# Attention, channel mix and gated MLP in one kernel: the output projection by seven block products, with sums on VectorE and GpSimd

## The chip, the cores and the metric

The kernel runs on one core of a Trainium2 chip. The metric is the device time in microseconds (us) of one execution, the median of several. TensorE multiplies, VectorE and ScalarE do the elementwise work and read TensorE's banks (PSUM), GpSimd does some elementwise work out of SBUF, and SyncE (SP) issues the DMAs.

## What is computed

Three layers, one behind the other, for 4 batches of 576 tokens (8 heads of 64, width 512, inner width 1024), all in FP32:

```python
# 1. causal attention with a forget bias
scores = q @ k.T / 8 + min(-(cum[:, None] - cum[None, :]), 0)   # cum: running sum of max(s, 0)
attn = exp(scores - rowmax);  attn /= attn.sum(-1) + 1e-9
x = attn @ v                                    # heads side by side: 4 x 576 x 512
# 2. channel mix (x_prev: the token before)
xk = mu_k * x + (1 - mu_k) * x_prev;  xr = mu_r * x + (1 - mu_r) * x_prev
x = sigmoid(xr @ w_r) * (relu(xk @ w_k) ** 2 @ w_v)
# 3. gated MLP
h = gelu_tanh(x @ w_in);  u, v = split(h)       # 512 and 512
v_n = (v - mean) / sqrt(var + 1e-6) * g_ln
v_s = w_sg @ v_n + b_sg                         # over the 576 tokens
out = x + (u * v_s) @ w_out
```

## The kernel before

**Precision.** A product in FP32 is made of three in a reduced form: each operand is split into a high half (a cast, mostly on ScalarE, `copy` at L71) and a low half (operand less high half, mostly on VectorE, `minus` at L74), and TensorE adds high by high, low by high and high by low in one PSUM bank (`mm3` L687, `mm3_steps` L674). Activations have channels on the 128 partitions and tokens along the row, and a tile of 288 tokens (half a batch, `HD`) is what one matmul streams: 128x128 weights, 288 columns.

**Attention and channel mix** run woven into each other up to about 510 us. `attend()` is a generator over 20 jobs, a job being two heads; `moe1()` is one over eight units of 288 tokens. The main loop takes steps of attention in proportion to the matmuls that `moe1` has given out. Both give their work priorities, and a scheduler that runs ahead of time sets each engine's order by them, so the order on an engine isn't that of the code. In attention, `scores` (products L359, L360) puts out scores that VectorE reduces to a row's extreme (L374) and ScalarE exponentiates (L400); `values` transposes, splits the result (`pth` on ScalarE, L545, `ptl` on VectorE, L546) and multiplies by the values (`av`, L527). For the twelve later jobs the division by the row sums comes last: `reciprocals` (L479) adds 1e-9 on GpSimd, inverts on VectorE and sends the row to DRAM, `spread` (L491) fetches it over 128 partitions by DMA (`rb`), and `scale` (L507) multiplies the job's 128x576 output `xt` by it on VectorE, one operation. `mix` (L599) then reads `xt`, first on ScalarE (L610). In `moe1` a unit makes keys (`wk`), the receptance (`wr`, with a tanh on ScalarE into `rt`, L651), turns it into a sigmoid by 0.5 * rt + 0.5 on VectorE (L657) and multiplies by `wv`'s products (L663). The result goes to DRAM (`x2_d`).

**The last stage** has four batches, in a fixed order by code (L975 to L988): `v_side` (v in token rows, GELU, mean and variance), the projection of the batch before, `u_side` (u in channel rows), `norm`, loading x of the next batch (`x_load`), `gate`. The projection of the last batch stands alone at the end. `gate` multiplies the normalised v by the spatial weights (`wg`, with 14 matmuls of 288 columns for each of eight blocks: 4 channel groups d, 2 token halves), scales and adds a bias on VectorE (L930), multiplies by u (L931) and splits into `gh` and `gl`. `project` (L936) makes eight outputs of 128 channels x 288 tokens; each takes 12 matmuls, 4 channel groups by 3, then a VectorE addition of x (L943) and a store. The weights `w_out` are converted from DRAM words to the two halves (`convert` L105, four pieces, bit operations on VectorE) between the first `norm` and the first `x_load` in the code (L982). PSUM in this stage is six banks, used in turn (`ps_b`, L842).

Of the kernel before, what the change touches and what calls it, by code (L numbers as in the profile page):

```python
# [22 lines left out]
P = 128  # L23
# [22 lines left out]
ENG = {"ia": "P", "mx": "D", "ca": "D", "p0": "P", "cl": "D", "qh": "D", "ql": "D", "kh": "A", "kl": "D", "vh": "A", "vl": "D", "xh": "A", "xl": "D", "fh": "A", "fl": "D", "rs": "D", "bh": "A", "bl": "D", "nh": "D", "nl": "D", "gh": "A", "gl": "D"}  # L46
# [6 lines left out]
def block_kernel(ctx: ExitStack, tc: tile.TileContext, qkv, vb, s, w_r, w_k, w_v, mu, w_in, w_out, w_sgT, g_ln, b_sg, out):  # L53
# [51 lines left out]
    def convert(w, c, n, t):  # L105
# [11 lines left out]
        nc.vector.scalar_tensor_tensor(ti, lw, 29, ti, ALU.logical_shift_right, ALU.bitwise_or)  # L117
        half = pool.tile([P, 2, 512], F32R, tag=name, name=name)
        copy("A" if att is not None else "D", half[:, 0], t)
        minus(ENG["cl"], half[:, 1], t, half[:, 0])  # L120
# [386 lines left out]
    def scale(w):  # L507
        nc.vector.tensor_tensor(w.xt[:, 1:], w.xt[:, 1:], w.rb, ALU.mult)
# [87 lines left out]
    def moe1():  # L596
# [29 lines left out]
        for u in range(2 * B):  # L626
# [30 lines left out]
            (nc.gpsimd if ENG["rs"] == "P" else nc.vector).tensor_scalar(rt, rt, 0.5, 0.5, ALU.mult, ALU.add)  # L657
            tc.cur_priority -= PM
            for m in range(4):
# [3 lines left out]
                nc.vector.tensor_tensor(rt[:, m], pm[:, 0:HD], rt[:, m], ALU.mult)  # L663
# [136 lines left out]
    def x_load(b):  # L800
        pool = pb if b % 2 else w2
        xf = pool.tile([P, 4, S], F32, tag="xf", name="xf")
        for hf in range(2):
            nc.sync.dma_start(xf[:, :, hf * HD : (hf + 1) * HD], x2_d[b][hf])
# [4 lines left out]
        xs[b] = xf, xh, xl, x4  # L809
        yield  # L810
        for c in range(4):
            copy(ENG["bh"], xh[:, c], xf[:, c])
            minus(ENG["bl"], xl[:, c], xf[:, c], xh[:, c])
            yield
        copy("D", x4[:, :, 0:D], xf[:, :, 4 * P :])
        minus("D", x4[:, :, D:], xf[:, :, 4 * P :], x4[:, :, 0:D])
# [3 lines left out]
    for size in moe1():  # L820
# [17 lines left out]
        if att is None and w2 is None:  # L838
# [5 lines left out]
            temps = w2.tile([P, 5, 512], F32, tag="vt", name="cvt")  # L844
            lws = conversions([(wi, c, n) for n in (1, 0) for c in range(4)], lambda i: temps[:, i % 5])
# [104 lines left out]
    for c, tags in enumerate(SLOTS):  # L950
# [11 lines left out]
        for x in range(2):  # L962
            wg[x].append(halves[x])
# [82 lines left out]
```

## Time and profile before

| | us |
|---|---|
| median of 3 runs | 701.81 |
| those runs, lowest and highest | 699.28, 704.09 |
| the profiled execution | 701.87 |
| its span, first to last instruction | 700.0 |
| TensorE busy in the span | 666.8 |
| VectorE busy | 535.2 |
| ScalarE busy | 425.0 |
| GpSimd busy | 33.1 |

The span is what the rows of the trace are counted in; the execution's own time is a little longer. The mean granted clock of TensorE is 0.992 of full speed. PE is TensorE's matmuls, PEld its weight loads (they overlap), DVE is VectorE, ACT ScalarE, POOL GpSimd, SPq the queue of SP. L12 is line 12 of the kernel.

### The profile page before, as it was taken

Reading aid. Unit: us, or ns where it says so; the run is one execution under the profiler, and the core shown is the slowest. Engines: PE = TensorE matmul, PEld = TensorE weight load, DVE = VectorE, ACT = ScalarE, POOL = GpSimd, SP = SyncE. Lnnn points to the kernel's source line nnn. Section 1 sums busy time; section 2 is a strip of 40 time slices with the busy share of each in tenths; the row PEclk is TensorE's granted clock in tenths of the full one; section 3 lists DMA queues with packets and bytes.
Section 4 is the critical chain, followed back from the end, with each engine's and each line's share of the span. In section 5 each row is a group of like instructions: output and inputs, shape, how many; then the busy total and the mean of one; then the engine's idle time right before and its main releaser. Section 6 shows DMA issues by size and latency. Waiting matters only on the chain.

```text
span 700.0 us, 12906 instructions
## 1 busy us (share of the span) xinstructions
PE 666.8 (95%) x4638; PEld 620.8 (89%) x4638; DVE 535.2 (76%) x1341; ACT 425.0 (61%) x1011; POOL 33.1 (5%) x86
## 2 busy tenths in 40 slices
PE   7799888999998999999999999999999999999998
PEld 4578866988888989988999999999998998998997
DVE  8999899898989899899887796743847564564543
ACT  5789797778868986896895745725523233133120
POOL 6122100000000000000000000000000000000000
PEclk9999999999999999999999999999999999999999
DMA  8894442352443333423202700004240300300101
GB/s 267 238 286 152 148 137 63 92 154 80 126 118 101 90 109 93 133 81 108 85 22 79 272 10 35 1 18 163 67 112 18 119 1 15 122 2 9 60 1 68
DMA packets 39831, 67.47 MB, mean 96 GB/s; under 512 B 6908, under 2 KB 23400, under 8 KB 39736
## 3 DMA queue, kind: packets, MB, share of 16 engines
q1 hardware_dynamic: 39768, 66.66, 31.2%
q8 instruction: 36, 0.59, 0.4%
q14 instruction: 27, 0.22, 0.1%
HBM read 51.85 MB, written 10.19 MB: 89 GB/s over the span
## 4 chain that ended last, share of the span: by engine, by line
PE 64%; DVE 19%; ACT 6%; DMA 4%; issue 3%; SPq 2%; DVEq 0%; POOL 0%; ACTq 0%
PE m L677 25%; PE po L690 7%; PE pu L690 7%; DVE pr L374 3%; PE pg L925 2%; PE pg L926 2%; PE pg L924 2%; DMA rb<-rd 2%; DVE qk L74 2%; PE pv L863 2%; PE pv L862 2%; PE pv L861 2%; PE av L527 2%; DVE ptl L546 2%; ACT pr L400 2%
## 5 line engine op out<-in xcount | busy, mean ns | idle before, releaser
L400 ACT ACTIVATE pr<-pr,nm 128x448 f32<-128x448 f32 (+4 forms) x144 | 85.1, 592 | 21.2 <-DVE nm L374 20.6
L677 PE MATMUL m<-xh,wk 128*128 128x288 f32 x512 | 83.2, 301 | 0.0
L677 PE MATMUL m<-kh,wv 128*128 128x288 f32 x512 | 79.1, 297 | 0.0
L677 PEld LDWEIGHTS m<-xh,wk 128*128 128x128 f32 x512 | 73.1, 191 | 1.8 <-ACT xh L71 0.7
L677 PEld LDWEIGHTS m<-kh,wv 128*128 128x128 f32 x512 | 71.5, 188 | 0.4
L374 DVE CUSTOM_DVE_ANT_0 pr<-s,mask 128x448 f32<-128x448 f32 (+4 forms) x144 | 64.9, 453 | 8.3 <-PE s L360 6.5
L359 PE MATMUL s<-qk 128*128 128x288 f32 (+4 forms) x144 | 46.8, 327 | 8.6 <-DVE nh L374 5.9
L71 ACT CAST xh<-xf 128x288 fp32r<-128x288 f32 (+1 forms) x80 | 36.1, 480 | 22.7 <-DVE xf L616 10.7
L677 PE MATMUL m<-xl,wk 128*128 128x288 f32 x256 | 47.4, 301 | 0.0
L545 ACT CAST pth<-t 128x512 fp32r<-128x512 f32 (+1 forms) x72 | 38.2, 532 | 13.4 <-PE t L542 12.3
L360 PE MATMUL s<-qk 128*128 128x288 f32 (+4 forms) x144 | 44.1, 309 | 1.8 <-DVE kl L74 1.8
L546 DVE TENSOR_TENSOR ptl<-t,pth 128x512 fp32r<-128x512 f32 (+1 forms) x72 | 43.9, 614 | 2.2 <-ACT pth L545 1.9
L677 PE MATMUL m<-kl,wv 128*128 128x288 f32 x256 | 44.2, 299 | 0.0
L638 ACT ACTIVATE kf<-m 128x288 f32<-128x288 f32 x64 | 26.2, 411 | 28.7 <-PE m L677 28.2
L74 DVE TENSOR_TENSOR xl<-xf,xh 128x288 fp32r<-128x288 f32 (+1 forms) x80 | 39.0, 508 | 5.7 <-PE m L677 4.2
L71 ACT CAST gh<-gf 128x288 fp32r<-128x288 f32 x32 | 13.9, 433 | 45.8 <-DVE gf L931 45.8
L542 PE MATMUL t<-ident,pr 128*128 128x128 f32 x252 | 40.0, 277 | 1.6 <-DVE ptl L546 1.0
L677 PE MATMUL m<-xh,wr 128*128 128x288 f32 x256 | 40.8, 298 | 0.5 <-ACT kf L638 0.3
L610 ACT ACTIVATE xf<-xt,mu 128x288 f32<-128x288 f32 x64 | 33.4, 535 | 12.2 <-DVE xl L74 8.3
L690 PE MATMUL pu<-xh,wi 128*128 128x288 f32 x256 | 39.9, 295 | 0.0
L690 PE MATMUL po<-gh,wk 128*128 128x288 f32 x256 | 39.3, 296 | 0.0
L359 PEld LDWEIGHTS s<-qk 128*128 128x128 f32 x144 | 27.3, 190 | 12.9 <-DVE nh L374 8.1
(299 smaller groups left out, 1738.9 us busy)
## 6 DMA issues: line engine op xcount, KB each, us to landing
kld<-qkv SPq DMA_DIRECT2D x28, 288.0 KB
qld<-qkv SPq DMA_DIRECT2D x24, 288.0 KB
x_d<-rt SPq DMA_DIRECT2D x8, 576.0 KB
xf<-x_d SPq DMA_DIRECT2D x8, 576.0 KB
outT<-ot SPq DMA_DIRECT2D x32, 144.0 KB
vld<-qkv SPq DMA_DIRECT2D x24, 160.0 KB
qk<-qk SPq DMA_DIRECT2D x24, 144.0 KB
rb<-rd SPq DMA_DIRECT2D x24, 128.0 KB
```

What stands on the lines that cost most here:

```text
L71: nc.scalar.copy(dst, src) if eng == "A" else nc.vector.tensor_copy(dst, src)
L74: (nc.gpsimd if pick(engines) == "P" else nc.vector).tensor_tensor(dst, a, b.bitcast(F32), ALU.subtract)
L359: nc.tensor.matmul(dst, qk[0][:, 0, qs], qk[0][:, 1, ks], start=True, stop=False)
L360: issued[0] = nc.tensor.matmul(dst, qk[1][:, 0, qs], qk[1][:, 1, ks], start=False, stop=True)
L374: nc.vector.tensor_tensor_reduce(out=dst, in0=src, in1=msk, scale=-0.125, scalar=first, op0=ALU.add, op1=ALU.min, accum_out=acc)
L400: i = nc.scalar.activation(dst, dst, AF.Exp, bias=nm[:, col : col + 1], scale=-1.0, accum_out=w.sm[:, col : col + 1])
L542: issued[0] = nc.tensor.transpose(bank[:, o : o + P], x, ident)
L545: nc.scalar.copy(pth[:, cols], bank[:, 0:o])
L546: nc.vector.tensor_tensor(ptl[:, cols], bank[:, 0:o], pth[:, cols].bitcast(F32), ALU.subtract)
L610: nc.scalar.mul(xf, xp, mu1[:, j, c : c + 1])
L677: i = nc.tensor.matmul(dst, w(x, c, m), xx[:, c], start=(n + c == 0), stop=(n == 2 and c == w.nk - 1))
L690: nc.tensor.matmul(dst, w(x, c, m), xx[:, c], start=(n + c == 0), stop=(n == 2 and c == w.nk - 1))
```

## The change

- **Projection.** The 512 channels of the gated tile are taken as two halves, its 576 tokens as two halves, and the 512 outputs as two halves: a 2x2 by 2x2 block product. It is made with seven block products instead of eight (Winograd's form): `p11`, `p12`, `p22` and four with sums of weights (`s1` to `s4`). A block product has 256 channels, 256 outputs and 288 tokens, 2 row blocks x 6 matmuls. `quarters` assembles `w_out`, folds the sums of weights once and splits them; it stands behind the first `gate` in the code. `gate` makes the differences of gated blocks (`less`) and splits them too (`halves`, into `tp`). The sums of products are additions on VectorE (`add`) out of PSUM. x is fetched once more for each output, by DMA, into five rotating `ot` tiles; the first addition to it is on GpSimd, and in the last batch's second row block on VectorE. In the last batch x is fetched whole into `xr`. The projection of batch 0 moves behind `u_side`, `norm` and `x_load` of batch 1; those of batches 1 and 2 stay where they were.
- **Norm.** The square root's activation and its table loads go. A bit trick and three Newton steps on VectorE take their place. The casts of the normalised v (`nh`) move from VectorE to ScalarE, as does the cast for `x4`.
- **Receptance.** `wv` is split at half its value, the operation at L657 goes, and the product becomes (rt + 1) * pm, one operation with three operands on VectorE. The GELU table is asked for ahead of time, once.
- **Softmax scaling.** `scale` runs on GpSimd.
- **Loading x.** `x_load` fetches half a batch at a time into one buffer, and converts two channel groups at once; the spatial weights of the last two token groups are loaded behind the first `u_side` instead of ahead of the stage.

```diff
 def convert(w, c, n, t):            # its first part is now assemble(w, c, n, t)
-        copy("A" if att is not None else "D", half[:, 0], t)
-        minus(ENG["cl"], half[:, 1], t, half[:, 0])
+        if w is wv:
+            nc.scalar.mul(half[:, 0], t, 0.5)
+            nc.vector.scalar_tensor_tensor(half[:, 1], t, 0.5, half[:, 0].bitcast(F32), ALU.mult, ALU.subtract)
...
     def scale(w):
-        nc.vector.tensor_tensor(w.xt[:, 1:], w.xt[:, 1:], w.rb, ALU.mult)
+        nc.gpsimd.tensor_tensor(w.xt[:, 1:], w.xt[:, 1:], w.rb, ALU.mult)
...
-            (nc.gpsimd if ENG["rs"] == "P" else nc.vector).tensor_scalar(rt, rt, 0.5, 0.5, ALU.mult, ALU.add)
...
-                nc.vector.tensor_tensor(rt[:, m], pm[:, 0:HD], rt[:, m], ALU.mult)
+                nc.vector.scalar_tensor_tensor(rt[:, m], rt[:, m], 1.0, pm[:, 0:HD], ALU.add, ALU.mult)
...
     def x_load(b):
+        for hf in range(2):
+            hs = slice(hf * HD, (hf + 1) * HD)
+            xf = w2.tile([P, 4, HD], F32, tag="xf", name="xf")
+            nc.sync.dma_start(xf, x2_d[b][hf])
             yield
+            for c in (slice(0, 2), slice(2, 4)):
+                copy(ENG["bh"], xh[:, c, hs], xf[:, c])
+                minus(ENG["bl"], xl[:, c, hs], xf[:, c], xh[:, c, hs])
+                yield
...
     def norm(b, vt, mv):
-        nc.scalar.activation(rs, var, AF.Sqrt)
-        nc.vector.reciprocal(rs, rs)
+        nc.vector.tensor_scalar(rs.bitcast(I32), var.bitcast(I32), 1, 0x7FFFFFFF, ALU.logical_shift_right, ALU.bitwise_xor)
+        nc.vector.tensor_scalar(rs, rs, 0.33885 * 2.0**-64, None, ALU.mult)
+        for _ in range(3):
+            nc.vector.tensor_tensor(t1, rs, rs, ALU.mult)
+            nc.vector.scalar_tensor_tensor(t1, t1, -0.5, var, ALU.mult, ALU.mult)
+            nc.vector.scalar_tensor_tensor(rs, t1, 1.5, rs, ALU.add, ALU.mult)
...
     def gate(b, ut, vh, vl, v4):    # behind the scale and bias of each block (d, hf)
+                if d < 2 and hf:
+                    nc.vector.tensor_tensor(tf[:, 0, c], gf, ut[d // 2][:, d % 2, hs], ALU.mult)
+                    less(tf[:, 1, c], tf[:, 0, c], last)
+                    halves(1, c, tf[:, 1, c])
+                    continue
+                nc.vector.tensor_tensor(gf, gf, ut[d // 2][:, d % 2, hs], ALU.mult)
+                if d >= 2:
+                    if hf:
+                        less(tf[:, 1, c], gf, tf[:, 1, c])
+                        less(tf[:, 0, c], gf, tf[:, 0, c])
+                    else:
+                        less(tf[:, 1, c], gf, tf[:, 1, c])
                 copy(ENG["gh"], gh[:, d, hs], gf)
                 minus(ENG["gl"], gl[:, d, hs], gf, gh[:, d, hs])
+                if d >= 2:
+                    for k, x in ((2, 1), (3, 0)) if hf else ((4, 1),):
+                        halves(k, c, tf[:, x, c])
+                last = gf
...
-    def project(b, xf, gh, gl):     # the eight outputs, 12 matmuls each
+    def project(b, gh, gl):
+        def part(a, x):
+            dst = ps_b.tile([P, 512], F32, tag="b", name="p" + a)[:, 0:HD]
+            for y, z in ((0, 0), (1, 0), (0, 1)):
+                for c in range(2):
+                    nc.tensor.matmul(dst, wq[a][:, y, c, ms], x[z][c], start=(n == 0), stop=(n == 5))
...
+        def emit(i, hf, u, bank):
+            if last:
+                ot = xr[:, i, hs]
+            else:
+                ot = pool.tile([P, HD], F32, tag="ot", name="ot", bufs=n)
+                nc.sync.dma_start(ot, x2_d[b][hf][:, i])
+            (nc.vector if last and m else nc.gpsimd).tensor_tensor(ot, ot, u, ALU.add)
+            add(ot, ot, bank)
+            nc.sync.dma_start(out[b, i * P : (i + 1) * P, hs], ot)
+
+        for m in range(2):
+            ms = slice(m * P, (m + 1) * P)
+            u1, u2 = place(0), place(1)
+            nc.scalar.copy(u1, part("11", block(0, 0)))
+            add(u2, u1, part("s2", tp[2]))
+            emit(m, 0, u1, part("12", block(1, 0)))
+            u3 = place(2)
+            add(u3, u2, part("s3", tp[3]))
+            p5 = part("s1", tp[1])
+            emit(2 + m, 1, u3, p5)
+            add(u2, u2, p5)
+            emit(m, 1, u2, part("s4", block(1, 1)))
+            emit(2 + m, 0, u3, part("22", tp[4]))
...
     for b in range(B):
         vt, mv = v_side(b, xh, xl, x4)
-        if b:
+        if b > 1:
             project(*tail)
...
+        if b == 1:
+            project(*tail)
         gh, gl = gate(b, ut, vh, vl, v4)
+        if b == 0:
+            quarters(last)
```

The order of instructions shows it at three places. The first is VectorE in attention, around a scaling of one of the last full jobs, before (`xt` is the job's output, `rcp` the reciprocals of the next):

```order
L74 TENSOR_TENSOR xl<-xf,xh 128x288
L374 ISA pr_91,nh<-s,mask 128x288
L374 ISA nh 128x1
L508 TENSOR_TENSOR xt_3630<-xt_3630,rb 128x576
L483 RECIPROCAL rcp<-sm 128x9
L74 TENSOR_TENSOR xl<-xf,xh 128x288
```

The same stretch of VectorE in the changed kernel, where L492 is the reciprocal, L383 the reduction and L555 the low half of the transposed scores:

```order
L492 RECIPROCAL rcp<-sm 128x9
L74 TENSOR_TENSOR xl<-xf,xh 128x288 x2
L74 TENSOR_TENSOR kl<-kf,kh 128x576
L555 TENSOR_TENSOR ptl<-t,pth 128x384
L383 ISA pr_91,nh<-s,mask 128x288
L383 ISA nh 128x1
```

The scaling is gone from VectorE; on GpSimd it alternates with the additions of 1e-9 to the row sums, and nothing else stands there in this stretch.

The second place is TensorE at the start of the last batch's projection, before, with the last matmul of the gate ahead:

```order
L928 MATMUL pg<-wg_6338,v_8223 128x288
L690 MATMUL po<-gh,wk_6601 128x288
L690 MATMUL po<-gh,wk_6609 128x288
L690 MATMUL po<-gh,wk_6617 128x288
```

These go on to 96. In the changed kernel `p_` is a product with a plain quarter of the weights, `ps_` one with a sum, and `tp` and the `wg` operands hold the split differences:

```order
L955 MATMUL pg<-wg_6551,v_8408 128x288
L988 MATMUL p_8611<-gh,w_6829 128x288 x4
L988 MATMUL p_8611<-gl,w_6829 128x288 x2
L988 MATMUL ps_8619<-tp,ws_6851 128x288
L988 MATMUL p_8627<-gh,w_6832 128x288
L988 MATMUL ps_8637<-wg_6305,ws_6844 128x288
L988 MATMUL ps_8645<-gh,ws_6839 128x288 x4
L988 MATMUL ps_8645<-gl,ws_6839 128x288 x2
L988 MATMUL ps_8656<-gh,ws_6848 128x288 x4
L988 MATMUL ps_8656<-gl,ws_6848 128x288
L988 MATMUL ps_8619<-tp,ws_6851 128x288 x3
```

There are 84 of them, and products whose operands are ready early are taken ahead of those on the last differences.

The third place is VectorE's end, before:

```order
L931 TENSOR_TENSOR gf<-gf,ut 128x288
L74 TENSOR_TENSOR gl<-gf,gh 128x288
L943 TENSOR_TENSOR ot<-po,xf 128x288 x8
```

and in the changed kernel, where L993 is an addition out of PSUM and L1014 one in SBUF:

```order
L1014 TENSOR_TENSOR xr<-xr,us 128x288 x2
L993 TENSOR_TENSOR xr<-ps_8710,xr 128x288
L993 TENSOR_TENSOR us<-ps_8710,us 128x288
L993 TENSOR_TENSOR xr<-p_8731,xr 128x288
L1014 TENSOR_TENSOR xr<-xr,us 128x288
L993 TENSOR_TENSOR xr<-ps_8721,xr 128x288
```

Eight additions became chains of additions, the last of which need the sum made just ahead of them.

## Rows read from the trace of the kernel before

**Rows 1.** The page: busy us (share) and instructions; the chain by engine.

```profile
PE 666.8 (95%) x4638; PEld 620.8 (89%) x4638; DVE 535.2 (76%) x1341; ACT 425.0 (61%) x1011; POOL 33.1 (5%) x86
...
PE 64%; DVE 19%; ACT 6%; DMA 4%; issue 3%; SPq 2%; DVEq 0%; POOL 0%; ACTq 0%
```

**Rows 2.** Busy time by stretch: length; PE, PEld, DVE, ACT, POOL; clock; DMA; GB/s.

```profile
120.00:385.00 265.00, 253.97 (x1835) 239.62 (x1836) 234.03 (x602) 212.20 (x537) 7.32 (x20) 1.00 0.33 98
583.00:636.00 53.00, 53.00 (x361) 50.46 (x360) 30.02 (x70) 14.99 (x29) 0.00 (x0) 1.00 0.14 46
```

**Rows 3.** The chain of waits in order of time, at its end: start, us, what.

```profile
683.89 12.81 PE po L690 x96
696.73 0.46 DVE ot L943
```

**Rows 4.** Waits of PE, 120 to 385 us: idle us, how often, the longest.

```profile
PE s L359 <- DVE nh L374: 5.9, 8, 1.7
...
PE av L527 <- DVE ptl L546: 2.7, 4, 1.6
```

**Rows 5.** Line L508: shortest/mean/longest ns, first and last; waits before; who waits.

```profile
L508 DVE TENSOR_TENSOR xt<-xt,rb x12: 751/760/764, 144.6 to 386.2; 128x576 f32<-128x576 f32 x12
...
  DMA rb<-rd: 4.3, 7
...
  ACT xf L610: 3.7, 3
```

**Rows 6.** Timeline of VectorE and TensorE around two scalings: start, us, what, [idle before].

```profile
166.24 0.76 DVE L508 TENSOR_TENSOR xt<-xt,rb 128x576 f32<-128x576 f32 x1 [0.68 <-DMA rb<-rd]
...
167.53 0.44 PE L527 MATMUL av<-ptl,vv 128*128 128x384 f32 x1 [0.53 <-DVE ptl L546]
...
302.22 0.76 DVE L508 TENSOR_TENSOR xt<-xt,rb 128x576 f32<-128x576 f32 x1 [0.82 <-DMA rb<-rd]
...
303.93 0.39 PE L527 MATMUL av<-ptl,vv 128*128 128x256 f32 x1 [1.55 <-DVE ptl L546]
```

**Rows 7.** Lines L657 and L663, as rows 5.

```profile
L657 DVE TENSOR_SCALAR rt<-rt x8: 702/751/762, 127.5 to 493.9; 128x1152 f32<-128x1152 f32 x8
...
L663 DVE TENSOR_TENSOR rt<-m,rt x32: 396/456/459, 131.8 to 505.9; 128x288 f32<-128x288 f32 x32
```

**Rows 8.** Lines by form on GpSimd: busy us, mean ns | idle before, by whom.

```profile
L482 POOL TENSOR_SCALAR sm<-sm 128x9 f32<-128x9 f32 x12 | 5.9, 492 | 206.3 <-ACT pr L400 206.3
...
L454 POOL TENSOR_SCALAR pr<-pr,rc 128x128 f32<-128x128 f32 x4 | 4.1, 1014 | 5.0 <-DVE rc L412 3.1 <-PE t L472 1.3 <-PE t L438 0.6
...
L74 POOL TENSOR_TENSOR qk<-qld,qk 64x256 fp32r<-64x256 f32 x4 | 3.5, 890 | 20.1 <-DMA vb<-vb 8.0 <-issue 6.1 <-ACT qk L71 6.0
```

**Rows 9.** Timeline of GpSimd and VectorE, 54 to 61 us.

```profile
54.97 1.88 POOL L74 TENSOR_TENSOR qk<-qld,qk 64x256 fp32r<-64x256 f32 x2 [7.98 <-DMA vb<-vb]
...
56.18 1.21 DVE L117 SCALAR_TENSOR_TENSOR cvt<-wr20w,cvt 128x512 int32<-128x512 int32 x1
...
59.90 0.68 DVE L117 SCALAR_TENSOR_TENSOR cvt<-wr30w,cvt 128x512 int32<-128x512 int32 x1
```

**Rows 10.** Timeline of VectorE in a gate of the last stage.

```profile
525.70 0.45 DVE L931 TENSOR_TENSOR gf<-gf,ut 128x288 f32<-128x288 f32 x1
526.07 0.51 DVE L930 SCALAR_TENSOR_TENSOR gf<-pg,g_sb,b_sb 128x288 f32<-128x288 f32 x1
526.65 0.46 DVE L74 TENSOR_TENSOR gl<-gf,gh 128x288 fp32r<-128x288 f32 x1
```

**Rows 11.** Lines of ScalarE, 385 to 700 us, as rows 8.

```profile
L894 ACT ACT_TABLE_LOAD x4 | 5.1, 1283 | 0.1
```

**Rows 12.** Timeline of VectorE, SP's queue and ScalarE at loads of x.

```profile
516.60 0.29 DVE L71 CAST x<-xf 128x256 fp32r<-128x256 f32 x1 [10.22 <-DMA xf<-x_d]
...
606.88 1.20 SPq L804 DMA_DIRECT2D xf<-x_d  x2
...
613.18 2.40 ACT L71 CAST xh<-xf 128x576 fp32r<-128x576 f32 x4 [1.85 <-DMA xf<-x_d]
```

More of the change, by code (lines that the diff above doesn't have):

```diff
@@ L656, in moe1 @@
             tc.cur_priority += PM
-            (nc.gpsimd if ENG["rs"] == "P" else nc.vector).tensor_scalar(rt, rt, 0.5, 0.5, ALU.mult, ALU.add)
+            if not more:
+                nc.scalar.activation(first, rt[:, 3, 0:1], AF.Gelu_apprx_tanh)
             tc.cur_priority -= PM
@@ L852, in v_side @@
     def v_side(b, xh, xl, x4):
-        vt = w2.tile([P, 5, DM], F32, tag="vt", name="vt")
+        vt = value_rows("vt")
         mv = mvs[b % 2]
@@ L880, in u_side @@
     def u_side(b, xh, xl):
-        ut = pb.tile([P, 4, S], F32, tag="ut", name="ut")
+        ut = [pb.tile([P, 2, S], F32, tag=f"ut{k}", name=f"ut{k}") for k in range(2)]
+        last = []
         for m in range(4):
@@ L913, in norm, with halves, less @@
         return vh, vl, v4
+    def halves(k, c, x):
+        copy("A", tp[k][0][c], x)
+        minus("D", tp[k][1][c], x, tp[k][0][c])
+    def less(dst, a, b):
+        nc.vector.tensor_tensor(dst, a, b, ALU.subtract)
     def gate(b, ut, vh, vl, v4):
@@ L948, in block_kernel, with spatial @@
         nc.gpsimd.memset(mv[:, 4], 1.0)
-    wg = [[], []]
-    for c, tags in enumerate(SLOTS):
+    wg, pieces = [[], []], []
+    def spatial(c, pool, tag, last=None):
+        tags = SLOTS[c]
         if len(tags) == 2:
-            halves = [w1p.tile([P, S], F32R, tag=t, name=f"wg{c}") for t in tags]
+            place = [w1p.tile([P, 1024], F32R, tag=t, name=f"wg{c}") for t in tags]
+            pieces.extend(x[:, S : S + HD] for x in place)
+            place = [x[:, 0:S] for x in place]
@@ L961, in block_kernel @@
-            minus("D", halves[1][:, hs], raw, halves[0][:, hs])
+            i = nc.scalar.copy(place[0][:, hs], raw)
+            if last is not None:
+                behind(i, last[7])
+            minus("D", place[1][:, hs], raw, place[0][:, hs])
         for x in range(2):
-            wg[x].append(halves[x])
+            wg[x].append(place[x])
+    for c in range(3):
+        spatial(c, mw, "xf")
     wo = Weight(w1p, "wk", w_out)
-    temps = w1p.tile([P, 2, 512], F32, tag="wk01", name="cvt")
@@ L966, in block_kernel, with quarters, split, fold @@
-    cos = conversions([(wo, i, 0) for i in range(4)], lambda i: temps[:, i % 2])
+    wq = {}
+    def quarters(last):
+        ta = w1p.tile([P, 2, 512], F32, tag="wk01", name="cvt")
+        tb = w1p.tile([P, 2, 512], F32, tag="wr30", name="cvt")
+        for c in range(4):
+            load_words(wo, c, 0)
+        for c in range(4):
+            assemble(wo, c, 0, (ta, tb)[c // 2][:, c % 2])
+        a11, a21, a12, a22 = (t[:, :, i * 256 : (i + 1) * 256] for t in (ta, tb) for i in range(2))
+        def split(name, pool, tag, x):
+            w = wq[name] = pool.tile([P, 2, 2, 256], F32R, tag=tag, name="w" + name)
+            behind(nc.scalar.copy(w[:, 0], x), last[5 if name[0] == "s" else 3])
+            minus("D", w[:, 1], x, w[:, 0])
+        def fold(dst, x, y, op):
+            nc.vector.tensor_tensor(dst, x, y, op)
+        split("11", w1p, "wk00", a11)
+        split("12", w1p, "wk10", a12)
+        split("22", w1p, "wk20", a22)
+        fold(a22, a21, a22, ALU.add)
+        split("s1", w1p, "wk30", a22)
+        fold(a21, a11, a21, ALU.subtract)
+        fold(a11, a22, a11, ALU.subtract)
+        split("s3", xtp, "xh", a21)
+        fold(a12, a12, a11, ALU.subtract)
+        split("s4", xtp, "xl", a12)
+        split("s2", w1p, "wr30", a11)
```

109 lines of the change are left out of this document (64 added, 45 removed).

## The prediction

> **What bounds the kernel now.** I read the page's busy shares and chain first, then busy times by stretch, then the waits of the stretch in which TensorE is not full. TensorE is busy 666.8 of 700.0 us and is 64% of the chain of waits, VectorE 19% [rows 1]. By stretch [rows 2] there are two kernels in one. In attention (120 to 385 us) TensorE is busy 254.0 of 265 us and VectorE 234.0: both are nearly full, and TensorE's 11 idle us there stand mostly behind VectorE (5.9 us before the scores, waiting for the reduction of the scores before them, 2.7 us before `av`) [rows 4]. From 385 us on TensorE is full and everything else is slack: in one batch of the last stage, 583 to 636 us, it is busy 53.00 of 53 us, VectorE 30.0, ScalarE 15.0, GpSimd 0. The projection there is one piece of the chain, 96 matmuls in 12.81 us, 0.1334 us each, and after the last of them stand only one VectorE addition of 0.46 us and its store [rows 3]. So in the last stage a matmul less is 0.133 us less, as long as nothing else becomes late; in attention what counts is VectorE's time.
>
> **The change part by part.** The sum is made against the profiled execution: span 700.0 us, 701.87 us as a whole, so 1.87 us lie around it; the median of the runs is 701.81 us, the same within 0.1 us.
>
> *Seven products for eight.* Before, one batch is 4 x 2 outputs of 12 matmuls, 96. After, it is 7 products x 2 row blocks x 6 matmuls, 84, of the same 128x128x288 form. 12 x 0.1334 = 1.60 us a batch, four batches: **-6.4 us**, if TensorE stays full.
>
> *What pays for it on VectorE, in the batches that are not the last.* The gate gets 14 more VectorE operations a batch (8 differences, 6 low halves), the projection 6 more (14 additions for 8). One 288-column operation follows another after 0.37 us (525.70 to 526.07), a scale-and-add after 0.58 us [rows 10]: 20 x 0.37 = 7.4 us. Newton's five more operations of 5 columns and the four casts that go to ScalarE about cancel. VectorE goes from 30.0 to some 38 us, TensorE from 53.0 to 51.4. That is still covered, with 13 us of slack. GpSimd gets 8 additions of 288 columns. Their price is not in the trace; nearest are 9 columns in 0.49 us on average and 64x256 in 0.89 us, both two plain forms [rows 8]; from these 288 columns take about 0.94 us (0.89 + 32 x 0.40/247), 7.5 us a batch. Even if VectorE stood still for all of it, it would have 45.5 us of 51.4. The cover is gone only beyond 5.9 us more. But a bank of PSUM is held until a GpSimd sum is there, and in these stretches single waits may come out: I take **+0.5 us** for three batches, 0 to 5 as bounds (0: all under the six banks; 5: each batch gives back its 1.6 us).
>
> *Batch 0.* The w_out conversion moves behind the gate in the code, and its four foldings and three more low halves come to VectorE; the order puts most of it still ahead of the gate's first result. Before, VectorE idles 10.22 us there, waiting for x. x now comes in two halves through one buffer, the second load only after the first is converted: before, in a later batch, both halves were issued by 608.1 us and converted from 613.18 us on [rows 12], so a load takes about 5 us and two in a row 10. The project of batch 0 is moved behind the second u-side, which leaves VectorE 12.8 us more. I cost it at nothing; the work that hides it is the gate's and v-side's 27 us of TensorE; without that cover it is up to 5 us, one load.
>
> *The square root.* Two table loads a batch of 1.283 us go [rows 11]; ScalarE is idle 38 of 53 us, so they are worth 0.
>
> *The last batch.* Here the cover ends. In the order rows TensorE issues 32 matmuls, 4.27 us, behind the gate before it needs the cast of the last gate block, and 53 matmuls, 7.1 us, before it needs the very last operand (`tp`, low). VectorE has 24 operations for the gate's second half, 20 x 0.37 + 4 x 0.58 = 9.7 us, and TensorE takes 56 x 0.133 = 7.5 us for it; VectorE can only start on each block when it is there, so it ends some 2.2 us late, plus two sums of `us` and the last block's own chain, about 5 us behind the gate's end for the last operand, 4.1 us for the cast. 4.1 against 4.27 us: just covered, and one GpSimd addition in between (0.94 us) uncovers it. Behind the last matmul there are now three VectorE additions instead of one: 2 x 0.4 = 0.8 us more. I take 0.8 + 0.5 = **+1.3 us**, bounds +0.5 and +4.
>
> *Scaling and receptance in attention.* VectorE loses 12 scalings of 0.760 us (9.1 us) and 4.3 us of standing before them for the row sums' DMA [rows 5], and eight `rt` operations of 0.751 us, six of them before 385 us (4.5 us); 24 of the 32 products with `rt` become the three-operand form, by the rows 0.52 for 0.456 us, +1.5 us [rows 7, 10]. That is 16.4 us of VectorE's 234, if GpSimd took nothing from it. It does take something: during the second of two GpSimd subtractions, 1.88 us together, a VectorE operation that otherwise takes 0.68 us took 1.21 us [rows 9], 0.53 us more for 0.94 us of GpSimd, about half. A 576-column scaling on GpSimd costs, from 0.89 us at 256 and 0.49 at 9 columns, 1.41 us; the lower bound is 0.89 us, the upper one, by the 128-column operation with a row's scalar (1.014 us), 4.6 us. I take 1.5, since it is the same plain form as the 0.89 us row. If VectorE stands half of it again, 12 x 0.75 = 9 us come back, and 7.4 us are left. What of it reaches TensorE is read from single places: after the scaling at 302.22 us (0.82 us wait) TensorE idles 1.55 us before `av`, after that at 166.24 us 0.53 us [rows 6]. These 2.1 us go, and of the other 9 us idle behind VectorE I take a tenth: **-3 us**. Bounds: -8 (nearly all of that idle time goes) and +7 (below).
>
> The Trainium skill says of this, in "SBUF — State Buffer" (SBUF: two separate sides), that GpSimd and VectorE share a pair of SBUF ports, and that whichever starts first holds it for its whole instruction against a VectorE operation with two SBUF inputs or in a two-port mode. The stretched row agrees. By that rule a scaling can hold VectorE for all of its 1.5 us and not for half, and the sum in attention would be 1.6 us of VectorE's time lost where I have 7.4 us won, or about 0 us in place of -3.
>
> *Sum.* 700.0 - 6.4 + 0.5 + 1.3 - 3.0 = 692.4 us span, + 1.87 = **694.3 us**, 1.1% under the median.
>
> **The rivals.**
> (A) As summed, 694.3 us, own range 691 to 698. For it: TensorE's full stretches and the counted matmuls.
> (B) VectorE is the real bound of attention, and all the relief reaches TensorE: -8 instead of -3, 689.3 us. For it: nearly all of TensorE's idle time there is behind VectorE. Against: after a removed wait the next engine (ScalarE, 212 of 265 us busy) is close.
> (C) The hold eats the relief in attention: 0 instead of -3, 697.3 us.
> (D) The last stage gives the projection's gain back, PSUM banks waiting for GpSimd's sums behind VectorE's norm: +5 instead of +0.5, 698.8 us. Against: 13 us of VectorE slack a batch.
> (E) Slower: the scaled tile comes late. GpSimd scales at twice or more my price, held up by VectorE as VectorE is by it. The mixing on ScalarE waited 3.7 us for three of the twelve scalings already [rows 5]. At 3 us a scaling these waits grow by 2.2 us each, 6.7 us over three, and VectorE loses 12 x 3.0 against 13.4 us won, 22 us, of which a third on the path is 7.5 us: -6.4 + 1.8 + 6.7 + 7.5 = +9.6, 711.5 us. It decides from about 2 us a scaling on; at 1.5 us it does not exist. Against: the 0.89 us row.
>
> **How the numbers follow.** About 1% (7 us) is what a measurement of this kernel can tell from no change. Chances: A 0.38, B 0.24, C 0.18, D 0.11, E 0.09. Faster by over 1% is under 694.8 us: B, and a little over half of A (0.22): 0.46. Slower is most of E: 0.07. The rest, 0.47, is the same. The predicted time is A's. The range reaches from B's, 1.3 us lower for the unknown in its size, to D's with 4 us for C and D together: 688 to 703; outside are E and the far end of B.
>
> **What would show it.** Of the changed kernel: TensorE at 84 matmuls a projection, 11.2 us, and no idle time in the last three batches but under 0.5 us each (D wrong). In the last batch under 1 us idle between the gate and the end, and three VectorE additions behind the last matmul. VectorE near 38 us in a batch. The GpSimd scalings at 1.3 to 1.7 us, and no VectorE wait for the row sums' DMA. TensorE's idle time from 120 us to the end of attention down from 11 to about 8 us, and attention over some 3 us earlier. I am wrong if the scalings take over 2 us, if the gaps in the last stage add up to more than 3 us, or if attention ends later than before.

## The result

| kernel | us, median (lowest to highest) | runs | against before, 95% interval |
|---|---|---|---|
| before, beside it | 700.96 (699.28 to 704.09) | 4 | |
| changed | 690.12 (689.22 to 694.87) | 4 | 0.9863 (0.9826 to 0.9899) |
| changed, again, beside experiments | 693.11 (690.91 to 695.70) | 4 | 0.9881 (0.9847 to 0.9915) |

The change takes 1.2 to 1.4% off, 9.5 us over the eight runs (median 692.0, against 701.5 over 43 further runs of before); 7.5 had been forecast. For the second four a median of 690 to 692 had been expected. The profiled execution of the changed kernel took 689.22 us, span 687.4 us.

One thing has to be known to read the numbers. One program's executions differ by up to 6 us, and most of it goes with TensorE's mean granted clock. In this profile it is 0.997, in that of before 0.992; before shows 0.94 in three of the first four stretches of 30 us, the changed kernel in one of them, and in the rest of both nearly all is at 1.00, the upper of its two levels (2.4 GHz). Over all runs of all kernels below, a line gives 3.5 us for 0.01 of mean clock. So below each kernel has, beside its median, its time on that line at a clock of 0.990. By that, before is 701.9 us (+-0.2) and the changed kernel 692.0 (+-0.4): 9.9 us. A +- is one standard error here and below. It leaves out that executions taken at different times differ by more than that: the two groups of four of the changed kernel lie 2.0 us apart on the line, and before, measured beside the last four kernels of the table below, 1.0 us under before beside the others. Differences of 1 to 2 us by the line alone are therefore weak; the times of whole stretches of the trace, below, are stronger.

The changed page, busy time and chain (as [rows 1]):

```profile
PE 654.9 (95%) x4590; PEld 612.5 (89%) x4590; DVE 563.2 (82%) x1412; ACT 436.3 (63%) x1058; POOL 80.9 (12%) x126
...
PE 69%; DVE 13%; issue 5%; ACT 5%; DMA 5%; POOL 1%; SPq 1%; DVEq 0%; ACTq 0%; POOLq 0%
```

48 matmuls less, VectorE 28 us more, GpSimd 48 us more, and VectorE's share of the chain down from 19 to 13%. The two stretches of [rows 2] in the changed kernel:

```profile
120.00:385.00 265.00, 258.67 (x1892) 247.45 (x1891) 229.75 (x589) 212.83 (x540) 23.54 (x31) 1.00 0.34 99
583.00:636.00 53.00, 53.00 (x360) 50.27 (x359) 36.95 (x89) 16.25 (x35) 9.76 (x9) 1.00 0.22 68
```

In attention TensorE gets 1892 matmuls done where it had 1835, and idles 6.3 us where it had 11.0. In the last stage it is as full as before, with VectorE at 37 us of 53. What TensorE waits for in attention (120 to 385 us, as [rows 4]):

```profile
PE av L536 <- DVE ptl L555: 4.0, 8, 0.7
PE s L368 <- DVE nh L383: 0.8, 1, 0.8
PE av L536 <- ACT pth L554: 0.7, 2, 0.5
```

The wait ahead of the scores fell from 5.9 to 0.8 us, that ahead of `av` grew from 2.7 to 4.0. The scaling, on GpSimd (as [rows 5]):

```profile
L517 POOL TENSOR_TENSOR xt<-xt,rb x12: 1417/1430/2003, 142.8 to 378.0; 128x576 f32<-128x576 f32 x12
...
  DMA rb<-rd: 11.2, 7
...
  ACT xf L619: 2.2, 4
```

It takes 1.43 us, GpSimd and not VectorE stands before the row sums' DMA, and the mixing waits no more than before (2.2 us for 3.7). The product with three operands, (rt + 1) * pm, takes as long as the one with two did (0.45 us both). The end of the chain (as [rows 3]):

```profile
682.99 0.41 PE p L988 x3
683.41 0.02 issue
683.43 0.46 DVE xr L993
683.89 0.38 DVE xr L1014
684.27 0.02 issue
684.29 0.46 DVE xr L993
```

Three additions stand behind the last product, 1.32 us to the end of the last, against one of 0.46.

The projection can be read without the clock, since the stages from the first gate on run at 1.00 but for the last few microseconds. The line of the gate's high products gives the first and the last start, in the kernel before, the changed kernel and the one with eight products (below):

```profile
L924 PE MATMUL pg<-wg,vh x128: 288/295/300, 509.0 to 683.1; 128*128 128x288 f32 x128
```

```profile
L951 PE MATMUL pg<-wg,vh x128: 288/295/300, 501.1 to 671.3; 128*128 128x288 f32 x128
```

```profile
L949 PE MATMUL pg<-wg,vh x128: 288/295/300, 501.0 to 675.0; 128*128 128x288 f32 x128
```

From the first start to the end of the span (700.0, 687.4 and 691.7 us) that is 191.0, 186.3 and 190.7 us. Over all profiled kernels it is 190.7 to 192.2 us with eight products (five) and 185.3 to 186.8, mean 185.9, with seven (nine). The kernel with eight products has the other edits of the last stage, and they give next to nothing (190.7 for 191.0).

Attention and the rest of the channel mix can be read in the same way, since every kernel here has 3350 matmuls ahead of the first gate. The last 2500 of them, before and changed (from 151.2 and 149.1 us to the first gate; a matmul or two more overlap the edge of the window):

```profile
151.25:509.00 357.75, 346.96 (x2501) 331.03 (x2500) 290.34 (x710) 255.65 (x614) 5.45 (x16) 1.00 0.30 91
```

```profile
149.05:501.05 352.00, 344.84 (x2502) 331.55 (x2501) 282.56 (x690) 255.19 (x621) 21.09 (x27) 1.00 0.31 96
```

The same work takes 5.8 us less. So of the 12.6 us between the two spans, 5.8 lie in this stretch, 4.7 behind it and 2.1 ahead of it, where the granted clock differs.

### The profile page after: what moved, and what is told of

It reads as the page before. It is cut to its first block, busy times and chain, and to the rows that moved or that the text cites. A ratio compares the mean times of both kernels' runs of the same rounds, so it can differ in the third digit from the quotient of the medians.

```text
span 687.4 us, 13039 instructions
## 1 busy us (share of the span) xinstructions
PE 654.9 (95%) x4590; PEld 612.5 (89%) x4590; DVE 563.2 (82%) x1412; ACT 436.3 (63%) x1058; POOL 80.9 (12%) x126
## 4 chain that ended last, share of the span: by engine, by line
PE 69%; DVE 13%; issue 5%; ACT 5%; DMA 5%; POOL 1%; SPq 1%; DVEq 0%; ACTq 0%; POOLq 0%
PE m L687 28%; PE pu L700 7%; PE ps L988 3%; PE av L536 3%; PE t L551 2%; PE pg L952 2%; PE pg L953 2%; PE pg L951 2%; PE p L988 2%; PE pv L876 2%; PE pv L877 2%; PE pv L875 2%; DVE pr L383 2%; PE s L368 2%; PE s L369 2%
## 5 line engine op out<-in xcount | busy, mean ns | idle before, releaser
L383 DVE CUSTOM_DVE_ANT_0 pr<-s,mask 128x448 f32<-128x448 f32 (+4 forms) x144 | 64.7, 453 | 7.9 <-PE s L369 6.8
L1014 POOL TENSOR_TENSOR ot<-ot,u 128x288 f32<-128x288 f32 x24 | 24.8, 1043 | 246.7 <-ACT u L1021 225.9
L74 DVE TENSOR_TENSOR xl<-xf,xh 128x288 fp32r<-128x288 f32 (+1 forms) x80 | 41.8, 540 | 11.2 <-ACT xh L71 6.1
L555 DVE TENSOR_TENSOR ptl<-t,pth 128x512 fp32r<-128x512 f32 (+1 forms) x72 | 44.2, 616 | 2.2 <-ACT pth L554 1.6
L687 PEld LDWEIGHTS m<-xl,wk 128*128 128x128 f32 x256 | 38.1, 189 | 0.3
L687 PEld LDWEIGHTS m<-xh,wr 128*128 128x128 f32 x256 | 36.2, 188 | 2.0 <-ACT kf L647 1.3
```

The source lines that it names most:

```text
L74: (nc.gpsimd if pick(engines) == "P" else nc.vector).tensor_tensor(dst, a, b.bitcast(F32), ALU.subtract)
L383: nc.vector.tensor_tensor_reduce(out=dst, in0=src, in1=msk, scale=-0.125, scalar=first, op0=ALU.add, op1=ALU.min, accum_out=acc)
L555: nc.vector.tensor_tensor(ptl[:, cols], bank[:, 0:o], pth[:, cols].bitcast(F32), ALU.subtract)
L687: i = nc.tensor.matmul(dst, w(x, c, m), xx[:, c], start=(n + c == 0), stop=(n == 2 and c == w.nk - 1))
```

## The experiments

All runs in one table; "idle" is TensorE's idle time from 120 to 390 us in the profile, which holds all of attention in its later part. In half of the profiles the granted clock is 1.00 in all of that stretch; in the other half it is 0.83 to 0.97 in one to four stretches of 10 us. "2500 matmuls" is the time of the last 2500 matmuls ahead of the first gate, less what such stretches cost (1 less the granted clock, times 10 us: 3.4 us in "before + both", the second changed one and "four pieces", 1.7 in "scaling back", "first additions" and "behind each scaling", 0 in the others). It is one execution each; the two of the changed kernel agree within 0.2 us, but where two kernels have one order of instructions in attention (below) they differ by up to 1.3.

| kernel | median us (runs) | at clock 0.990 | idle us | 2500 matmuls us |
|---|---|---|---|---|
| before | 701.5 (43) | 701.9 | 11.0 | 357.8 |
| before + scaling on GpSimd | 699.85 (10) | 700.7 | 10.0 | 356.2 |
| before + half folded into wv | 700.92 (10) | 701.4 | 9.9 | 357.5 |
| before + both | 698.83 (10) | 698.2 | 6.8 | 352.4 |
| changed | 692.0 (8) | 692.0 | 6.3, 6.5 | 352.0, 351.8 |
| changed, scaling back on VectorE | 694.48 (4) | 693.9 | 9.0 | 356.2 |
| changed, receptance as before | 696.32 (5) | 695.4 | 9.2 | 356.3 |
| changed, eight products | 697.41 (7) | 695.5 | 6.8 | 352.6 |
| changed, first additions on VectorE | 692.07 (4) | 692.4 | 6.5 | 352.0 |
| changed, GpSimd operation behind each scaling | 693.91 (4) | 693.9 | 8.2 | 355.3 |
| changed, GpSimd operation ahead of each scaling | 695.02 (4) | 693.5 | 9.1 | 355.4 |
| changed, scaling in four pieces | 695.23 (4) | 693.7 | 7.2 | 353.5 |
| changed, q's low halves on GpSimd too | 690.87 (4) | 689.0 | 6.0 | 350.7 |

The standard error of a value at 0.990 is 0.4 us for ten runs and 0.6 for four.

**The parts of attention, one by one.** The scaling alone, in the kernel before:

```diff
-        nc.vector.tensor_tensor(w.xt[:, 1:], w.xt[:, 1:], w.rb, ALU.mult)
+        nc.gpsimd.tensor_tensor(w.xt[:, 1:], w.xt[:, 1:], w.rb, ALU.mult)
```

> The kernel before, with the softmax scaling alone moved to GpSimd. In the changed kernel the last stage begins 8.1 us earlier than before (first v_side product at 396.5 for 404.6 us). Theory 1, VectorE's time is the bound of attention: the scaling takes 9.1 us of work and 4.3 us of waits off VectorE and gives 4.4 us back where GpSimd's scaling holds it, 9.0 us net of the 12.0 us that the whole change takes off it there, so three quarters of the 8.1 us: the last stage begins 6 us earlier, total about 695. Theory 2, only the waits for the row sums' DMA count: 4.3 us earlier at most, total about 697. Theory 3, the gain is that of a new order that the scheduler happened on, and not of the scaling: no fixed sign, within 2 us of 701.

Measured: 0.9989 of before (0.9968 to 1.0009), 1.2 us at the same clock. Not the 6 us of theory 1. The waits of TensorE, 120 to 390 us, tell where they went:

```profile
PE av L527 <- DVE ptl L546: 5.3, 11, 1.2
PE s L359 <- DVE nh L374: 1.6, 2, 0.8
PE av L527 <- ACT pth L545: 1.4, 4, 0.7
```

The wait ahead of the scores is gone (1.6 for 5.9 us), and the one ahead of `av` has grown by most of that (5.3 for 2.7, and ScalarE's part 1.4 for 0.3). It moved. The longest of these waits, 1.20 us, with VectorE's queue ahead of it:

```profile
311.70 0.81 DVE L74 TENSOR_TENSOR xl<-xf,xh 128x288 fp32r<-128x288 f32 x2
312.44 0.74 DVE L657 TENSOR_SCALAR rt<-rt 128x1152 f32<-128x1152 f32 x1
313.10 0.74 DVE L74 TENSOR_TENSOR qk<-kld,qk 64x576 fp32r<-64x576 f32 x1
313.77 0.68 DVE L546 TENSOR_TENSOR ptl<-t,pth 128x512 fp32r<-128x512 f32 x1
...
314.50 0.39 PE L527 MATMUL av<-ptl,vv 128*128 128x256 f32 x1 [1.20 <-DVE ptl L546]
```

VectorE comes to `ptl` without a gap, and one of the operations ahead of it is the receptance's `rt`. The fold that removes that one, alone (with `wv` split at half its value in `convert`, as in the change):

```diff
-            (nc.gpsimd if ENG["rs"] == "P" else nc.vector).tensor_scalar(rt, rt, 0.5, 0.5, ALU.mult, ALU.add)
...
-                nc.vector.tensor_tensor(rt[:, m], pm[:, 0:HD], rt[:, m], ALU.mult)
+                nc.vector.scalar_tensor_tensor(rt[:, m], rt[:, m], 1.0, pm[:, 0:HD], ALU.add, ALU.mult)
```

> The kernel before, with the receptance's half folded into wv alone (no operation of 0.751 us a unit, three operands in the product). Theory 1, VectorE's time is the bound: it takes 3.0 us net off VectorE in attention, a quarter of the whole, so the last stage begins 2 us earlier, total about 699. Theory 2, only waits count: no wait is removed, 0 us, total 701. Theory 3, a new order: any sign, as large as for the scaling.

Measured: 0.9992 (0.9969 to 1.0016), 0.5 us at the same clock. The scores' wait is as it was (5.2 us). Both together in the kernel before:

> The kernel before with both edits of attention, the scaling on GpSimd and the receptance's half folded into wv; last stage as before. Alone they gave 1 us (699.85 for 701.7) and nothing that can be told (700.9), where 6 and 2 had been expected, and yet TensorE's idle time from 120 to 400 us is 11.0 us before, 6.3 in the changed kernel and 6.8 in the one with eight products. Theory 1, VectorE's time counts, but the two edits only tell together: 5 to 6 us faster than before, about 696, idle 120 to 400 us near 6.5 us. Theory 2, the gain ahead of 400 us belongs to the rest of the change (conversions and loads taken out of the way): about 700, idle near 10 us. Theory 3, to the order that the scheduler found: any of the two, but then the two kernels of the same call that undo one edit each lose as much for reasons of order.

Measured: 0.9961 (0.9937 to 0.9986), 3.7 us at the same clock, idle 6.8 us. Its waits:

```profile
PE av L531 <- DVE ptl L550: 3.5, 7, 0.8
PE av L531 <- ACT pth L549: 1.0, 2, 0.9
PE s L363 <- DVE nh L378: 0.8, 1, 0.8
```

Each alone gives about 1 us of idle time, both 4.2; of the 2500 matmuls' time 1.6 and 0.3 us, both 5.4. Now the same from the other end, the changed kernel with one of them undone (the diffs above, backwards).

> The changed kernel with the softmax scaling back on VectorE. Theory 1 (VectorE's time, both edits needed): most of the gain in attention goes, 4 to 5 us slower than the changed kernel, about 695. Theory 2 (the rest of the change): within 1.5 us of the changed kernel, about 691. Theory 3 (order): between the two, with the loss at single waits of TensorE that do not stand behind the scalings.

Measured: 694.48 us, 1.9 us (+-0.7) slower than the changed kernel at the same clock, idle 9.0 us, the 2500 matmuls 4.2 us longer.

> The changed kernel with the receptance as before: wv split at its whole value, 0.5 * rt + 0.5 as an operation of its own on VectorE, two operands in the product. Theory 1: up to 5 us slower than the changed kernel, about 695 (both edits needed) or 2 us (VectorE's time by its share). Theory 2 (the rest of the change): within 1.5 us, about 691. Theory 3 (order): any value up to 5 us slower.

Measured: 696.32 us, 3.4 us (+-0.7) slower, idle 9.2 us, the 2500 matmuls 4.3 us longer. The waits of these two, in that order:

```profile
PE s L368 <- DVE nh L383: 5.1, 6, 1.7
PE av L536 <- DVE ptl L555: 2.1, 3, 1.1
```

```profile
PE av L532 <- DVE ptl L551: 5.1, 11, 1.2
PE av L532 <- ACT pth L550: 1.6, 3, 1.1
PE s L364 <- DVE nh L379: 1.6, 2, 0.8
```

They are the waits of the two single edits again: with the scaling on VectorE TensorE waits at the scores, with `rt` there and the scaling gone it waits at `av`. That both edits are needed is shown, and theory 2 (the rest of the change) falls: with both in the kernel before, the 2500 matmuls take 352.4 us, as in the changed kernel. Theory 3 (order) is not ruled out by this. The order of instructions on TensorE, VectorE, ScalarE and GpSimd is the same, record for record, up to some 400 us in "before + scaling" and "receptance as before", in "before + fold" and "scaling back", and in "before + both" and "eight products", so that the same waits in both families are no second piece of evidence. The fold alone hardly changes the order before (of 1099 VectorE operations ahead of the first gate 1059 stand in the same sequence), the scaling changes it much (797). How much of the gain is VectorE's time and how much the order that goes with it, these runs don't separate; the kernel with a GpSimd operation behind each scaling (below) has the changed kernel's order on TensorE and VectorE through attention, and there time lost on VectorE is seen to reach TensorE.

**The projection.** Eight products in blocks of 12 matmuls, one addition on VectorE each, nothing else changed:

> The changed kernel with eight block products of 12 matmuls an output and one addition on VectorE for each (no differences in the gate, no sums of weights, no addition on GpSimd); everything else as changed. By the two traces the seven products give 3.7 us over the first three batches and 0.8 us at the end, 4.5 us. If the projection is what does that, this kernel is 4.5 us slower than the changed one, about 694.6 us, with the loss only behind the first v_side, and its attention ends within 1 us of the changed kernel's. Rival: the projection gives next to nothing and the last stage owes its time to the other edits there (norm, loading of x): under 1.5 us slower, about 691.

Measured: 697.41 us, 3.5 us (+-0.6) slower than the changed kernel at the same clock, and 4.4 us by the stages of the two profiles (190.7 for 186.3 us), none of it ahead of the first gate (501.0 and 501.1 us). The 4.5 us hold; against the mean of the nine profiles with seven products (185.9 us) it is 4.8 us. Then where the first addition to x runs:

```diff
-            (nc.vector if last and m else nc.gpsimd).tensor_tensor(ot, ot, u, ALU.add)
+            nc.vector.tensor_tensor(ot, ot, u, ALU.add)
```

> The changed kernel with the first addition to x of each output on VectorE in place of GpSimd, in all batches. Theory, GpSimd's additions cost nothing and save nothing because VectorE has slack in the first three batches: within 1 us of the changed kernel, about 690. Rival, GpSimd's additions (1.04 us each, 24 of them) hold VectorE and PSUM banks: 1 to 2 us faster. Second rival, VectorE becomes late without GpSimd's help: the three projections lose up to 1.6 us each, 2 to 5 us slower.

Measured: 692.07 us, 0.4 us slower at the same clock, less than can be told. From 583 to 636 us TensorE is full either way, VectorE at 37.3 us instead of 37.0. GpSimd's additions neither cost nor save.

**What GpSimd does to VectorE.** In the changed kernel, one scaling beside reductions and low halves that read PSUM, and one beside a low half whose two operands are both in SBUF:

```profile
142.80 1.43 POOL L517 TENSOR_TENSOR xt<-xt,rb 128x576 f32<-128x576 f32 x1 [1.12 <-DMA rb<-rd]
...
142.98 0.51 DVE L383 CUSTOM_DVE_ANT_0 pr<-s,mask,nh 128x288 f32<-128x288 f32 x1
...
143.88 0.68 DVE L595 TENSOR_TENSOR p<-t,p 64x512 fp32r<-64x512 f32 x1 [0.38 <-ACT p L594]
```

```profile
338.03 0.75 DVE L74 TENSOR_TENSOR qk<-kld,qk 64x576 fp32r<-64x576 f32 x1
338.08 2.00 POOL L517 TENSOR_TENSOR xt<-xt,rb 128x576 f32<-128x576 f32 x1 [17.64 <-DVE xt L584]
338.82 1.87 DVE L74 TENSOR_TENSOR kl<-kf,kh 128x576 fp32r<-128x576 f32 x1
...
341.21 0.38 PE L536 MATMUL av<-ptl,vv 128*128 128x256 f32 x1 [0.52 <-DVE ptl L555]
```

The first pair doesn't notice one another: 0.51 and 0.68 us are what these operations always take. In the second, VectorE's `qk` starts first and the scaling takes 2.00 us instead of 1.43; then `kl`, which takes 0.75 us elsewhere, lasts 1.87 us and ends 0.6 us behind the scaling, and TensorE waits 0.52 us behind the queue. Four VectorE operations in the twelve scalings were stretched, by 4.4 us in all, every one with two SBUF operands; three of the eight `av` waits (1.8 of 4.0 us) stand right behind one. In the eleven profiles with the scaling on GpSimd, of the VectorE operations from 120 to 390 us that began in a GpSimd multiplication, addition or subtraction of two tiles with 0.3 us or more of it to go, all 66 with two SBUF operands were stretched, and none of the 179 that read PSUM. To test it, one more GpSimd operation behind each scaling:

```diff
         nc.gpsimd.tensor_tensor(w.xt[:, 1:], w.xt[:, 1:], w.rb, ALU.mult)
+        nc.gpsimd.tensor_tensor(w.rb, w.rb, w.rb, ALU.mult)
```

> The changed kernel with one more GpSimd operation right behind each of the twelve scalings: the 128x576 tile of reciprocals is multiplied by itself (1.43 us by the scalings' row, nothing reads the result). It costs nothing but what it does to VectorE. In the changed kernel four VectorE operations that read two SBUF operands were stretched by 1.0 to 1.2 us while a scaling ran, and none of those that read PSUM. Theory 1, one such operation at a time stands still for the rest of the GpSimd operation: some four more are stretched by about 1.1 us, and TensorE's idle time from 120 to 390 us goes from 6.2 to 7 to 8 us; total 1 to 2 us slower. Theory 2, GpSimd slows VectorE by half for as long as it runs (as I had priced it): no operation by over 0.8 us, all kinds alike, total about 3 us slower. Theory 3, no effect: idle 6.2 us.

Measured: 693.91 us, 1.9 us (+-0.7) slower at the same clock, idle 8.2 us. Ten operations are stretched by 8.0 us in all, again only ones with two SBUF operands; of the six more four lost 0.4 to 0.5 us, since they met the end of the 1.15 us operation, and two 0.9 and 1.0. Theory 1, with a smaller price for most. The order through attention is the changed kernel's, VectorE loses 3.6 us more, and the 2500 matmuls take 3.4 us longer (1.7 of clock already taken off): with the order fixed, most of what VectorE loses here reaches TensorE. The same operation ahead of the scaling instead:

> The changed kernel with that operation ahead of each scaling, so that the scaled tile comes 1.43 us later at 2.9 us a scaling (the output is scaled by the square of the reciprocal). It prices rival E: by it the waits of the mixing on ScalarE for the scaled tile (2.2 us for four of them in the changed kernel) grow by 1.4 us each and reach TensorE, with VectorE's loss 6 us or more slower than the changed kernel. Theory, the lateness is hidden: as the kernel with the operation behind the scaling, 0 to 2 us slower.

Measured: 695.02 us, 1.5 us (+-0.7) slower at the same clock, and the 2500 matmuls 355.4 us, like its sibling (355.3). The mixing's waits for the scaled tile went from 2.2 to 4.2 us, not by 1.4 each, and idle is 9.1 us. The lateness is mostly hidden. Four pieces of 144 columns:

> The changed kernel with each scaling in four operations of 144 columns on GpSimd. If a stretched VectorE operation waits for the end of the GpSimd operation that is running, the longest stretch goes from 1.1 to under 0.6 us, and TensorE's idle time from 120 to 390 us from 6.2 to about 5.5 us; the total is within 1 us of the changed kernel. Rival, GpSimd takes each following operation ahead of VectorE: stretches as long as before. Four operations may cost GpSimd 0.2 to 0.3 us each beyond their columns, 2.2 us for 1.43, and then tell as the late kernel does.

Measured: 695.23 us, 1.7 us (+-0.7) slower at the same clock. A piece takes 0.49 us, so 2.0 us a scaling. The stretches did shrink: those that are left are 0.3 us each or less. One of them, with the piece that it waited for:

```profile
345.21 1.06 POOL L519 TENSOR_TENSOR xt<-xt,rb 128x144 f32<-128x144 f32 x1 [1.41 <-DVE xt L586]
...
345.84 1.04 DVE L74 TENSOR_TENSOR kl<-kf,kh 128x576 fp32r<-128x576 f32 x1
```

But idle is 7.2 us, not 5.5: the mixing waits 5.3 us for the tile. What was won in one place was lost in another. Last, an attempt to go on along the same road:

```diff
-ENG = {... "ql": "D", ...
+ENG = {... "ql": "P", ...
```

> The changed kernel with the low halves of q of the twelve later jobs on GpSimd too (24 operations of 64x576, 0.76 us each on VectorE, 18 us in all). If VectorE's time is what TensorE's idle time in attention follows, and one GpSimd operation in three stretches a VectorE operation by 1.1 us (9 us), VectorE wins 9 us more: idle time from 120 to 390 us from 6.2 to about 4.5 us, 1 to 2 us faster. Rival, the low half of q comes late, since GpSimd takes about 1.4 us for it, and TensorE waits for it ahead of the scores: 1 to 3 us slower.

Measured: 690.87 us, 0.9854 of before (0.9825 to 0.9882), 3.0 us (+-0.7) faster than the changed kernel at the same clock, though idle is only 0.3 to 0.5 us less (6.0 us) and the intervals of the two against before overlap. At the same clock it is the fastest of these kernels. The 2500 matmuls take 1.3 us less than in the changed kernel, within the 1 to 2 us expected; the other 1.7 us are no more than the 2.0 us by which two groups of the changed kernel differ. The stretched operations rose to 23 and 15.9 us, 11.6 more where 9 had been put down, so VectorE won some 6 us net; it did not turn into the 1.7 us of idle time that I had expected from it.

## Why the prediction was right, point by point

**Seven products.** -6.4 us with +0.5 for banks and +1.3 at the end, -4.6 in sum. The stages gave 4.4 us against the kernel with eight products, 4.8 by the mean of all profiles with seven. The sum holds because two of its parts were off in opposite ways. The end costs 0.86 us (1.32 for 0.46): the two more additions as worked out, but not the 0.5 us for a GpSimd addition in the way (TensorE has no wait between the last gate and its last product). From the first gate to the end of the last product it is 187.7 us before (696.7 less 509.0) and 182.3 changed (683.4 less 501.1), 5.4 less; 6.4 less 0.5 would be 5.9. One wait of 0.4 us, for a copy on ScalarE in batch 0's projection, is the only one in the stage; the rest of that difference isn't at any single wait. Rival D, the stage giving it back, is out.

**VectorE in a batch** was put at 38 us; it is 37.0 from 583 to 636 us, and 41.5 in the batch with batch 0's projection. The cover held, the norm, the loads of x and the GpSimd additions cost nothing that shows.

**Attention** was put at -3 us, bounds -8 and +7. Idle time fell by 4.5 to 4.7 us and the 2500 matmuls by 5.8, 5.4 of it with the two edits alone: the sign is right, the forecast half of it. The row that I priced the scaling from (0.89 us for 256 columns) was the right one: 1.43 us for 1.41. Two steps below it were off. First, "VectorE stands half of it again", 9 us: it stood 4.4, because most of what VectorE does there reads PSUM, and the three-operand product put at +1.5 us cost nothing; VectorE won some 13 us where I had 7.4. The Trainium skill has the condition in "SBUF — State Buffer" (SBUF: two separate sides): only a VectorE operation with two SBUF inputs, or in a two-port mode, contends with GpSimd, and whichever starts first keeps the ports for its whole instruction. The trace agrees for two SBUF inputs and for both sides, 1.87 for 0.75 us on VectorE and 2.00 for 1.43 on GpSimd. I had used its whole length, which gave rival C, and left out how few operations meet the condition. Second, what of it reaches TensorE. The 2.1 us were to go from the `av` waits behind two scalings, and of the other 9 us a tenth. In fact the scores' wait nearly all went, 5.1 us, and 1.3 to 2.6 us came back ahead of `av`. Of the eight waits at the scores before, the two right behind a scaling make only 0.6 of 5.9 us. The longest stands behind low halves and a step of the mixing, with no scaling in the queue:

```profile
220.05 0.75 DVE L74 TENSOR_TENSOR qk<-qld,qk 64x576 fp32r<-64x576 f32 x1
220.83 0.75 DVE L74 TENSOR_TENSOR qk<-kld,qk 64x576 fp32r<-64x576 f32 x1
221.51 0.51 DVE L616 SCALAR_TENSOR_TENSOR xf<-xt,mu_sb,xf 128x288 f32<-128x288 f32 x1
221.94 0.44 DVE L374 CUSTOM_DVE_ANT_0 pr<-s,mask 128x288 f32<-128x288 f32 x1
...
222.44 0.47 PE L359 MATMUL s<-qk 128*128 128x448 f32 x1 [1.74 <-DVE nh L374]
```

I had looked for the gain right behind single scalings; it came from VectorE's queue as a whole, together with the new order. That attention's share came within its bounds and near enough to leave the total in its range is therefore in part luck.

**That it was the sum of two edits** was the step I did not see. I added the VectorE time of scaling and fold and turned it into idle time at one rate. Singly they give 1 us of idle time each, together 4.2.

**Rivals.** A is what happened, with the value nearer the middle between A and B: 692.0 us over eight runs, while the first four alone (690.1) lie just under A's own range and close to B. E (from 2 us a scaling on, slower) was run at 2.6 us and cost 1.5 us at the same clock, 3.4 by the 2500 matmuls, where the rival, at 3 us a scaling, had it 17 above A: the tile's lateness is hidden by the work that stands between scaling and mixing.

**What stays open.** At the same clock the kernel before with both edits takes 698.2 us and the changed one with eight products 695.5. The two have the same order of instructions on TensorE, VectorE, ScalarE and GpSimd through attention, the same idle time (6.8 us), 352.4 and 352.6 us for the 2500 matmuls and 191.0 and 190.7 from the first gate on. So the 2.7 us don't show from there on. The profiles point to the clock: the profiled execution of the former has a granted clock of 0.83 from 90 to 120 us and of 0.98 from 120 to 390, that of the latter 0.94 and 1.00, they reach the 2500 matmuls at 153.3 and 148.5 us, and the line counts a low clock the same wherever it falls. No run shows more. Open as well is how much of attention's gain is VectorE's time and how much the order.

## What to carry to other kernels

Where two engines are both nearly full, part of a wait that goes at one place can come back at the next: look at which wait stands behind it on the same engine, and cost the edits together, not one by one. When work is moved to GpSimd, count not its length but how many VectorE operations with two SBUF operands run beside it; those that read PSUM go on untouched. Block products with fewer multiplications paid 4.4 to 4.8 of the 6.4 us that the count of matmuls gives, in a stage where TensorE was full and the sums found room elsewhere; 0.9 us of the difference is what they add behind the last product. Where executions differ by their clock, compare the time of the same count of instructions in stretches at full clock.

## What the runs showed of the hardware

GpSimd multiplying a tile by itself took 1.15 us where two different operands took 1.43, both 128x576. In the first 120 us of these programs the granted clock falls in single stretches of 10 us to between 0.57 and 0.99, at other places in each execution, and mostly from 10 to 30 and from 90 to 120 us, where TensorE is not kept full (busy 24.2 of 30 us from 90 to 120 us in the changed kernel, 24.4 before); further on it is 1.00 up to the last few microseconds in half of the profiles, and in the other half falls to 0.83 to 0.97 in one to four stretches of 10 us, all ahead of 230 us. In two executions of the changed kernel that goes with 4.5 us at the first gate (501.1 and 505.6 us).
